# A planner that keeps a clock for the DMAs, and splits a loaded piece of weights by it

## The chip, the cores and the metric

The kernel runs on one core of one Trainium2 chip. The metric is device time in microseconds (us) of one execution. Times of before come from three timed runs and one profiled execution.

## The reference, cut to what matters

Attention with a decaying bias over 8 batches of 8 heads (576 tokens, 64 per head), and then a mixture of 8 experts on its output, 4608 rows of 512:

```python
scores = where(causal, -1e9, q @ k.T / 8 + min(-(cum_i - cum_j), 0))   # cum = cumsum(max(s, 0))
x = softmax(scores) @ v                                                # 4608 x 512
# routing: all 4608*8 logits x @ w_gate in falling order; a token goes to the expert of its largest
# logit that still has room; an expert takes cap = 576 tokens
for e in range(8):
    out[mask_e] = max(x[mask_e] @ w1[e], 0) @ w2[e]      # w1[e] 512 x 1024, w2[e] 1024 x 512
```

The output is what counts; the gate's product must be exact enough that no token goes to another expert, so x and the weights are held as two f16 numbers each, a high part and a remainder.

## The kernel before, in words

The first part of the span (up to about 342 us) is attention; the change leaves it alone. Then experts follow one another, numbered here 1 to 8 in the order in which they fill up (the code's `j` is 0 to 7).

One expert computes in two halves. In the h half TensorE multiplies the gathered, transposed rows `xT` by `w1p` into `ph` (128x512, line 1109) and `pht` (128x64, line 1113): 96 pairs of one of each. ScalarE makes `hT` from it (line 1117), VectorE its remainder (1126). In the y half TensorE multiplies `hT` by `w2p` into `py` (lines 1146 and 1137), ScalarE copies `y` out (1148), and GpSimd writes it to the output by a scatter (`out_dram`, line 1158), five per expert.

While one expert computes, the next is prepared:

- The routing search and the places of its tokens, a chain of small VectorE instructions and small TensorE matmuls (`cnt`, lines 870 to 900) that goes back and forth between the two. It ends in `iw` (which rows of the weights) and `ids` (which rows of x).
- The weights come in 12 pieces by indirect DMAs that GpSimd issues (line 1051, tile `wst`): 4 of `w1` (128x1024 f32, 0.52 MB) and 8 of `w2` (128x512 f32, 0.26 MB). A piece is then split: ScalarE makes the high part (`hi`, line 1055), VectorE the remainder (`lo`, line 1059). There are four buffers for pieces of w1 and five for those of w2; a buffer is free after `lo`.
- The rows of x come by five indirect DMAs (`xg`, line 1075, the gathers), and each is turned by a transposing DMA that SyncE issues (`xT`, line 1078).

All engines take their instructions in a fixed order, which a planner writes while the program is built. `Clock` (line 1179) holds a planned time for TensorE (`t`), ScalarE, VectorE and GpSimd. `use(eng, dt)` adds work to an engine; `after(eng, dt, lag, f)` adds work and puts `f` on a list of things that are due `lag` later; `tick` moves `t` on with each matmul and calls what is due. What is called is recorded at that place of its engine's order, so due times set the order, and no instruction waits for a planned time on the chip: it waits for its data, its buffer, and the instructions ahead of it on its engine.

`load(j, k)` (line 1253) issues piece k of an expert and makes its `hi` due by line 1269: 1.25 us of GpSimd's planned time, and then `LAT = 7.5` us. `hi` puts the remainders on the list `spare`, from which the main loop takes one when VectorE has room. `fetch(j)` (line 1281) is asked between matmuls. It issues the five gathers when `ids` is there; else the next piece, if a buffer is planned to be free (line 1295). After the gathers it holds the w2 pieces of an expert that isn't computing yet for `HOLD = 11.0` us. `scatter` (line 1155) takes 1.1 us of GpSimd's planned time.

Of the kernel before, what the change touches and what calls it, by code (L numbers as in the profile page):

```python
# [55 lines left out]
class Attention:  # L56
    def __init__(self, tc, ctx, qT, kT, vN, sN, wg, xs, nb, L, router=None):
        self.router = router
        self.tc, self.nc = tc, tc.nc
        self.qT, self.kT, self.vN, self.sN, self.wg, self.xs, self.L = qT, kT, vN, sN, wg, xs, L  # L60
        self.nb = nb
        P = lambda name, bufs, **k: ctx.enter_context(tc.tile_pool(name=name, bufs=bufs, **k))
        self.P = P
        self.c = P("ac", 1)
        self.dr = P("adr", 1, space=DRAM)
        self.st = {}
# [643 lines left out]
SLATE = -1.0  # L710
PACE = 1.7
GPACE = 1.3
HOLD = 11.0
PLEAD = 0.7
LAT = 7.5
NW = (4, 5)
HOP = -0.6
AHEAD = 0.5
# [306 lines left out]
class Moe:  # L1025
# [62 lines left out]
    def units(self, xT, w1p, w2p, ids, clock, f0=0, turn=()):  # L1088


        nc = self.nc
        h = {}

        def start():
            h["h"] = self.p.tile([128, 8, 2, 512], F16, name="hT", bufs=1)
            h["r"] = self.p.tile([128, 8, 2, 64], F16, name="hR", bufs=1)
            h["t"] = self.ps_t.tile([128, 8, 64], F32, name="pht", tag="pt")

        def mm1(f, c, k, tiles=None):
            if "h" not in h:  # L1100
                start()
            if f not in h:
                h[f] = self.ps.tile([128, 4, 128], F32, name="ph", tag="ps")
            ph, pt = h[f], h["t"]
            a, b = ((0, 0), (0, 1), (1, 0))[k]
            w = w1p[:, c, a, 128 * f:128 * f + 128]
            first, last = c == 0 and k == 0, c == 3 and k == 2
            if tiles is None:
                nc.tensor.matmul(ph, w, xT[:, 0:4, 4 * b + c], start=first, stop=last)  # L1109
            elif tiles < 4:  # L1110
                nc.tensor.matmul(ph[:, tiles], w, xT[:, tiles, 4 * b + c], start=first, stop=last)  # L1111
            if tiles in (None, 4):
                nc.tensor.matmul(pt[:, f], w, xT[:, 4, 4 * b + c, 0:64], start=first, stop=last)  # L1113
            if last and tiles in (None, 3):
                hT = h["h"]
                p2 = ph.rearrange("p i t -> p (i t)")
                nc.scalar.activation(hT[:, f, 0], p2, AF.Relu)  # L1117
                clock.after("a", 0.45, RLATE, lambda: lo(p2, hT[:, f, 1], hT[:, f, 0]))
                if f == 7:
                    hR = h["r"]  # L1120
                    nc.scalar.activation(hR[:, :, 0], pt, AF.Relu)
                    clock.after("a", 0.45, RLATE, lambda: lo(pt, hR[:, :, 1], hR[:, :, 0]))

        def lo(ps, o, hi):
            clock.use("v", 0.65)
            nc.vector.scalar_tensor_tensor(o, ps, 0.0, hi, op0=OP.max, op1=OP.subtract)  # L1126

        def mm2(i, f, k):
            n = 128 if i < 4 else 64
            if i == f == k == 0:  # L1130
                h["y"] = self.p.tile([128, 5, DM], F32, name="y")
            if f == k == 0:
                h["py"] = self.ps.tile([128, DM], F32, name="py", tag="ps")
            py, hT, y = h["py"], h["h"], h["y"]
            if i == 4:

                nc.tensor.matmul(py, h["r"][:, f].rearrange("p a t -> p (a t)"), w2p[:, f, k],  # L1137
                                 start=(f == 0 and k == 0), stop=(f == 7 and k == 1))
                if f == 7 and k == 1:
                    t = self.p.tile([64, DM], F32, name="t")  # L1140
                    nc.scalar.activation(t, py[64:128], AF.Copy, scale=YSC)
                    clock.after("a", 0.45, 0.2, lambda: fold(y, py, t))
                return
            a, b = ((0, 0), (0, 1), (1, 0))[k]
            first, last = f == 0 and k == 0, f == 7 and k == 2
            nc.tensor.matmul(py, hT[:, f, a, 128 * i:128 * i + n], w2p[:, f, b], start=first, stop=last)  # L1146
            if last:
                nc.scalar.activation(y[:, i], py, AF.Copy, scale=YSC)  # L1148
                clock.after("a", 0.45, SLATE, lambda: scatter(y, n, i))

        def fold(y, py, t):
            nc.vector.scalar_tensor_tensor(y[:64, 4], py[0:64], YSC, t, op0=OP.mult, op1=OP.add)
            clock.after("v", 0.65, SLATE, lambda: scatter(y, 64, 4))

        def scatter(y, n, i):
            clock.use("p", 1.1)
            nc.gpsimd.memset(self.spacer, 0.0)
            st = nc.gpsimd.indirect_dma_start(  # L1158
                out=self.out, out_offset=bass.IndirectOffsetOnAxis(ap=ids[:n, i:i + 1], axis=0),
                in_=y[:n, i], in_offset=None)  # L1160
            for s in self.scat:
                self.tc.declare_no_dep(st.ins, s.ins, reason="other rows")
            self.scat.append(st)

        us = [(0.47, f) for f in turn[:1]]
        for i in range(5 if f0 else 0):
            us += [(0.47, f) for f in turn[i + 1:i + 2]]

            us += [(0.058 if i < 4 else 0.03, lambda i=i, f=f, c=c, k=k: mm1(f, c, k, i))
                   for ks in (((0, 1), (2,)) if i == 0 else (range(3),))  # L1170
                   for f in range(f0) for k in ks for c in range(4)]
        us += [(0.245, lambda f=f, c=c, k=k: mm1(f, c, k)) for f in range(f0, 8) for c in range(4) for k in range(3)]
        n1 = len(us)
        us += [(0.216, lambda i=i, f=f, k=k: mm2(i, f, k))
               for i in (0, 1, 2, 4, 3) for f in range(8) for k in range(3 if i < 4 else 2)]
        return us, n1


class Clock:


    def __init__(self):
        self.at = dict(t=0.0, a=0.0, v=0.0, p=0.0)
        self.late = []

    @property
# [4 lines left out]
    def use(self, eng, dt):  # L1191
        self.at[eng] = max(self.at[eng], self.t) + dt
        return self.at[eng]

    def after(self, eng, dt, lag, f):

        self.late.append((self.use(eng, dt) + lag, f))
# [17 lines left out]
def route_and_experts(tc, ctx, R, xs, w1, w2, out):  # L1215
# [3 lines left out]
    clock = Clock()  # L1219
# [33 lines left out]
    def load(j, k):  # L1253

        u = info[j]["wu"][k]

        def hi():
            clock.after("a", u[1](), 0.1, lambda: spare.extend(parts))

        def lo(i):  # L1260
            clock.use("v", u[2][i]())
            if i + 1 == len(u[2]):
                now["out"][k > 3] -= 1
                info[j]["left"].discard(k)

        parts = [lambda i=i: lo(i) for i in range(len(u[2]))]
        u[0]()
        now["out"][k > 3] += 1
        clock.after("p", 1.25, LAT, hi)


    spare = []
# [1 line left out]
    def wait():  # L1274

        if spare:
            spare.pop(0)()
        else:
            clock.wait()

    def fetch(j, force=False):

        d = info[j]
        if "weights" in d and "w1p" not in d:
            d["w1p"], d["w2p"], d["wu"] = M.weights(d["weights"])
            d["left"], d["next"] = set(range(12)), 0
        if "ids" in d and "xT" not in d:
            d["xT"], d["xu"] = M.gather(d["ids"])
        if d.get("xu"):
            for f in d["xu"]:  # L1290
                clock.use("p", GPACE)
                f()
            d["xu"], d["hold"] = [], clock.t + HOLD
            return GPACE * 5
        free = lambda: now["out"][d["next"] > 3] < NW[d["next"] > 3]

        early = j > now["j"] and (not d.get("hold") or clock.t < d["hold"])
        if "wu" in d and d["next"] < 12 and not (early and d["next"] > 3) and (free() or force):
            while not free():
                wait()  # L1300
            load(j, d["next"])
            d["next"] += 1
            return PACE
        return None
# [7 lines left out]
    d = info[0]  # L1312
# [20 lines left out]
    for j in range(E):  # L1333
        d = info[j]
# [22 lines left out]
        if j + 1 < E:  # L1357
            d = info[j + 1]
            while "ids" not in d:
                if not step(streams[1], True):  # L1360
                    step(streams[0], True)

            while d.get("xu", True) or d["left"] & set(range(4)):
                if not fetch(j + 1):
                    wait()
# [53 lines left out]
```

## Time and profile before

| | us |
|---|---|
| timed runs, median (lowest to highest) | 862.95 (859.68 to 864.87) |
| the profiled execution, its own time | 858.84 |
| its span, first to last instruction | 857.1 |
| TensorE busy in the span | 761.5 (89%) |
| VectorE, GpSimd, ScalarE busy | 613.0, 478.4, 387.0 |

The mean granted clock of TensorE is 0.942 of full speed. A row of a timeline gives start, duration, engine, line, operation, tiles and count, and in brackets the idle time before it and what ended it. PE is TensorE, DVE VectorE, ACT ScalarE, POOL GpSimd, SP SyncE.

### The profile page before, as it was taken

The page shows a single profiled execution, that of the slowest core. Times are in us where ns is not written, and L with a number is a line of the kernel's source. Part 1 is how long each engine was busy: PE and PEld are TensorE (multiplying, and loading weights), DVE is VectorE, ACT ScalarE, POOL GpSimd, SP SyncE. Part 2 cuts the span into 40 slices and gives each one's busy share as a digit, 9 for nine tenths or more (in the row PEclk, how much of TensorE's full clock was granted, in tenths as well). Part 3 has the DMA queues.
Part 4 walks back from the last instruction along what each step waited for, and adds up shares of the span by engine and source line. Part 5 has one row for each costly group of instructions (what it writes and reads, how often), then busy time and mean ns, then how long its engine had stood idle before and what let it go on. Part 6 is the DMA issues. An engine that isn't in the chain of part 4 may idle for free.

```text
span 857.1 us, 22612 instructions
## 1 busy us (share of the span) xinstructions
PE 761.5 (89%) x9241; PEld 482.7 (56%) x9241; DVE 613.0 (72%) x1578; ACT 387.0 (45%) x866; POOL 478.4 (56%) x587
## 2 busy tenths in 40 slices
PE   8887899989889998269989999998989969959996
PEld 3576777877777787147545455454444525424442
DVE  6789999999999978668768878776677737115110
ACT  5466778878768787024213333231232113214110
POOL 5577899999989996062353534633462342432101
PEclk9689999999999999589999999999998979969999
DMA  6865999898988806052393837546283290491001
GB/s 176 249 178 151 198 238 236 207 236 234 232 205 223 177 31 141 33 187 67 114 188 103 223 101 194 151 134 169 81 211 107 95 221 28 125 210 62 31 13 43
DMA packets 122222, 128.69 MB, mean 150 GB/s; under 512 B 79781, under 2 KB 88329, under 8 KB 122118
## 3 DMA queue, kind: packets, MB, share of 16 engines
q1 hardware_dynamic: 103938, 74.31, 37.1%
q0 software_dynamic: 15744, 52.46, 20.3%
q8 instruction: 72, 1.18, 0.6%
q10 hardware_dynamic: 2436, 0.48, 0.3%
q14 instruction: 32, 0.26, 0.1%
HBM read 71.99 MB, written 19.49 MB: 107 GB/s over the span
## 4 chain that ended last, share of the span: by engine, by line
PE 48%; DVE 24%; issue 12%; DMA 5%; POOL 5%; ACT 3%; another core or an unknown queue 1%; ACTq 0%; SPq 0%; POOLq 0%; DVEq 0%
PE py L1146 15%; PE ph L1109 15%; DVE mr L297 7%; DVE R L393 3%; PE pht L1113 2%; PE py L1137 2%; DVE K L267 2%; DVE Vl L267 2%; PE ph L1111 2%; PE cnt L883 2%; POOL R L393 2%; PE pi L1013 1%; DVE Q L267 1%; DMA md<-mt 1%; DMA Q<-Q 1%
## 5 line engine op out<-in xcount | busy, mean ns | idle before, releaser
L393 POOL TENSOR_TENSOR R<-P 128x512 f16<-128x512 f32 x158 | 195.9, 1254 | 19.3 <-ACT P L391 19.3
L1109 PE MATMUL ph<-xT,w1p 128*128 128x512 f16 x696 | 187.1, 391 | 11.8 <-issue 11.7
L1146 PE MATMUL py<-w2p,hT 128*128 128x512 f16 x768 | 177.1, 381 | 0.3 <-issue 0.3
L1051 POOL DMA_INDIRECT wst<-in_w_dram,iw x96 | 98.3, 1024 | 138.8 <-DVE iw L857 40.4
L1113 PE MATMUL pht<-xT,w1p 128*128 128x64 f16 x768 | 139.0, 195 | 8.9 <-issue 8.7
L297 DVE TENSOR_REDUCE mr<-pss 128x1 f32<-128x512 f32 (+4 forms) x224 | 133.5, 608 | 9.9 <-PE pss L305 5.7
L391 ACT ACTIVATE P<-pst 128x512 f32<-128x512 f32 (+1 forms) x224 | 120.5, 563 | 41.4 <-PE pst L384 14.6
L1158 POOL DMA_INDIRECT out_dram<-y,ids x40 | 42.7, 1068 | 155.9 <-ACT y L1148 127.2
L1109 PEld LDWEIGHTS <-w1p 128*128 128x128 f16 x696 | 69.5, 100 | 93.8 <-issue 22.5
L1146 PEld LDWEIGHTS <-hT 128*128 128x128 f16 x768 | 70.2, 98 | 81.5 <-issue 5.4
L1117 ACT ACTIVATE hT<-ph 128x512 f16<-128x512 f32 x64 | 38.1, 597 | 169.5 <-PE ph L1109 89.0
L459 PE MATMUL po<-V,R 128*128 128x65 f16 x960 | 112.9, 195 | 1.3 <-POOL R L393 1.0
L457 PE MATMUL po<-V,P 128*128 128x65 f16 x960 | 112.4, 196 | 0.9 <-DVE xf L479 0.9
L458 PE MATMUL po<-Vl,P 128*128 128x64 f16 x960 | 112.3, 194 | 0.0
L382 PE MATMUL pst<-Q,K 70*128 70x64 f16 (+4 forms) x512 | 104.7, 253 | 4.3 <-ACT P L391 3.0
L384 PE MATMUL pst<-Q,K 128*128 128x64 f16 (+4 forms) x512 | 105.4, 253 | 0.0
L1126 DVE SCALAR_TENSOR_TENSOR hT<-ph,hT 128x512 f16<-128x512 f32 x64 | 43.8, 687 | 84.9 <-ACT hT L1117 54.4
L457 PEld LDWEIGHTS <-P 128*128 128x128 bf16 x960 | 91.1, 99 | 5.6 <-issue 0.2
L303 PE MATMUL pss<-K,Q 67*128 67x512 f16 (+3 forms) x256 | 72.5, 311 | 22.8 <-DVE mr L297 19.6
L459 PEld LDWEIGHTS <-R 128*128 128x128 f16 x960 | 90.3, 98 | 1.8 <-POOL R L393 1.5
L458 PEld LDWEIGHTS <-P 128*128 128x128 bf16 x960 | 90.2, 100 | 1.1 <-issue 1.0
L1113 PEld LDWEIGHTS <-w1p 128*128 128x128 f16 x768 | 71.3, 99 | 12.9 <-issue 12.2
(223 smaller groups left out, 1562.7 us busy)
## 6 DMA issues: line engine op xcount, KB each, us to landing
rq<-in_q_dram SPq DMA_DIRECT2D x32, 288.0 KB
rk<-in_k_dram SPq DMA_DIRECT2D x32, 288.0 KB
rv<-in_v_dram SPq DMA_DIRECT2D x32, 288.0 KB
Q<-Q SPq DMA_DIRECT2D x62, 144.0 KB
K<-K SPq DMA_DIRECT2D x62, 144.0 KB
xs<-xp SPq DMA_DIRECT2D x32, 256.0 KB
wst<-in_w_dram,iw POOLq DMA_INDIRECT x96
xs<-xp SPq DMA_DIRECT2D x8, 128.0 KB
```

The lines of the kernel that those rows point to most:

```text
L297: nc.vector.tensor_reduce(o, ps, AX.X, OP.max)
L382: nc.tensor.matmul(ps[:, c0:c0 + n], K[0:70, 0, par, pr, ks], Q[0:70, 0, pr, par, q0:q0 + n], start=True, stop=False)
L384: nc.tensor.matmul(ps[:, c0:c0 + n], K[:, 1, par, pr, ks], Q[:, 1, pr, par, q0:q0 + n], start=False, stop=not diag)
L391: nc.scalar.activation(P[:, c0:c0 + n], ps[:, :n], AF.Exp, scale=1.0 / YS)
L393: self.post(lambda: eng.tensor_tensor(R[:, c0:c0 + n], P[:, c0:c0 + n], strided_hi(P)[:, c0:c0 + n], op=OP.subtract), T["RT"][0 if gp else 1])
L457: nc.tensor.matmul(po[:, i, :], H[:, c:c + 128], V[:, pr, sl, :], start=f, stop=False)
L458: nc.tensor.matmul(po[:, i, 0:64], H[:, c:c + 128], Vl[:, pr, sl, :], start=False, stop=False)
L459: nc.tensor.matmul(po[:, i, :], R[:, c:c + 128], V[:, pr, sl, :], start=False, stop=l)
L1051: nc.gpsimd.indirect_dma_start(out=t, out_offset=None, in_=src, in_offset=bass.IndirectOffsetOnAxis(ap=iw[:, k:k + 1], axis=0))
L1109: nc.tensor.matmul(ph, w, xT[:, 0:4, 4 * b + c], start=first, stop=last)
L1113: nc.tensor.matmul(pt[:, f], w, xT[:, 4, 4 * b + c, 0:64], start=first, stop=last)
L1146: nc.tensor.matmul(py, hT[:, f, a, 128 * i:128 * i + n], w2p[:, f, b], start=first, stop=last)
```

## The change

The planner gets a fifth clock, `d`, for the DMAs. Each piece, gather and scatter adds a cost to it: 2.6 us for a piece of w1, 1.4 for one of w2, 3.0 for a gather, 1.0 for a scatter, starting at 2.0 us after the planned time or when `d` is through with what came before. The `hi` of a piece is due at the later of two times: 6.0 us after the planned time at which it is issued, or 3.5 us after `d` is through with it. The hold after the gathers is 10.0 us in place of 11.0. No instruction is added or taken away; what changes is their order on the engines.

```diff
-HOLD = 11.0
+HOLD = 10.0
 PLEAD = 0.7
-LAT = 7.5
+LAT = (6.0, 3.5)
+DMA = dict(w1=2.6, w2=1.4, x=3.0, y=1.0)
...
         def scatter(y, n, i):
             clock.use("p", 1.1)
+            clock.dma("y")
...
-        self.at = dict(t=0.0, a=0.0, v=0.0, p=0.0)
+        self.at = dict(t=0.0, a=0.0, v=0.0, p=0.0, d=0.0)
...
+    def dma(self, what):
+
+        self.at["d"] = max(self.at["d"], self.t + 2.0) + DMA[what]
+        return self.at["d"]
...
         u[0]()
         now["out"][k > 3] += 1
-        clock.after("p", 1.25, LAT, hi)
+        clock.use("p", 1.25)
+        clock.late.append((max(clock.t + LAT[0], clock.dma("w2" if k > 3 else "w1") + LAT[1]), hi))
...
             for f in d["xu"]:
                 clock.use("p", GPACE)
+                clock.dma("x")
                 f()
             d["xu"], d["hold"] = [], clock.t + HOLD
```

Nine lines are added above some of the code, so line 1051 is 1052 in the new file, 1055 is 1056, 1075 is 1076, 1117 is 1118 and 1158 is 1160.

GpSimd while expert 4 computes and expert 5 is fetched: before,

```order
L1051 DMA wst<-in_w_dram,iw 128x1024 x4
L1075 DMA xg<-xs,ids 128x1024 x4
L1075 DMA xg<-xs,ids 64x1024
L1051 DMA wst<-in_w_dram,iw 128x512 x4
L1157 MEMSET spacer 1x1
L1158 DMA out_dram<-y,ids 4608x512
L1051 DMA wst<-in_w_dram,iw 128x512 x2
```

and in the changed kernel, at the same place of the same engine:

```order
L1052 DMA wst<-in_w_dram,iw 128x1024 x4
L1076 DMA xg<-xs,ids 128x1024 x4
L1076 DMA xg<-xs,ids 64x1024
L1052 DMA wst<-in_w_dram,iw 128x512 x2
L1159 MEMSET spacer 1x1
L1160 DMA out_dram<-y,ids 4608x512
L1052 DMA wst<-in_w_dram,iw 128x512 x3
```

Between the gathers and the first scatter of expert 4 stand two pieces of w2 in place of four; the others stand behind the scatter.

GpSimd while expert 6 computes and expert 7 is fetched: before,

```order
L1051 DMA wst<-in_w_dram,iw 128x1024 x2
L1075 DMA xg<-xs,ids 128x1024 x4
L1075 DMA xg<-xs,ids 64x1024
L1051 DMA wst<-in_w_dram,iw 128x1024 x2
L1051 DMA wst<-in_w_dram,iw 128x512 x3
L941 MEMSET X 128x40
L1051 DMA wst<-in_w_dram,iw 128x512 x2
L1157 MEMSET spacer 1x1
L1158 DMA out_dram<-y,ids 4608x512
```

and in the changed kernel:

```order
L1052 DMA wst<-in_w_dram,iw 128x1024 x4
L1076 DMA xg<-xs,ids 128x1024 x4
L1076 DMA xg<-xs,ids 64x1024
L1052 DMA wst<-in_w_dram,iw 128x512 x4
L942 MEMSET X 128x40
L1052 DMA wst<-in_w_dram,iw 128x512
L1159 MEMSET spacer 1x1
L1160 DMA out_dram<-y,ids 4608x512
```

Two pieces of w1 have moved from behind the gathers to in front of them: five pieces follow the gathers in place of seven.

ScalarE in the h half of expert 1 (`w2p` is a `hi`, `hT` an h tile): before,

```order
L1055 ACTIVATE w2p<-wst 128x512
L1117 ACTIVATE hT<-ph 128x512 x3
L1055 ACTIVATE w2p<-wst 128x512 x2
L1117 ACTIVATE hT<-ph 128x512
L1055 ACTIVATE w2p<-wst 128x512 x2
L1117 ACTIVATE hT<-ph 128x512
L1055 ACTIVATE w2p<-wst 128x512
L1117 ACTIVATE hT<-ph 128x512 x2
L1121 ACTIVATE hR<-pht 128x8x64
```

and in the changed kernel:

```order
L1056 ACTIVATE w2p<-wst 128x512
L1118 ACTIVATE hT<-ph 128x512 x2
L1056 ACTIVATE w2p<-wst 128x512
L1118 ACTIVATE hT<-ph 128x512
L1056 ACTIVATE w2p<-wst 128x512 x2
L1118 ACTIVATE hT<-ph 128x512
L1056 ACTIVATE w2p<-wst 128x512
L1118 ACTIVATE hT<-ph 128x512 x3
L1122 ACTIVATE hR<-pht 128x8x64
```

The last `hi` stands one h tile earlier than before.

## Rows read from the trace of the kernel before

**Rows 1.** The page's head, and the engines' busy time.

```profile
span 857.1 us, 22612 instructions
...
PE 761.5 (89%) x9241; PEld 482.7 (56%) x9241; DVE 613.0 (72%) x1578; ACT 387.0 (45%) x866; POOL 478.4 (56%) x587
```

**Rows 2.** Waits from 390 to 857 us: total us, times, longest.

```profile
PE cnt L891 <- DVE ca L887: 7.5, 5, 3.3
...
ACT w1p L1055 <- DMA wst<-in_w_dram,iw: 2.3, 1, 2.3
...
ACT w2p L1055 <- DMA wst<-in_w_dram,iw: 1.1, 1, 1.1
```

**Rows 3.** Windows, TensorE alone: the last h half, then four stretches of fetching.

```profile
core 0: us, PE busy (x), PEclk, DMA share, GB/s
803.00:823.00 20.00, 20.00 (x165) 1.00 0.04 14
583.00:589.00 6.00, 3.45 (x19) 0.90 1.15 301
638.00:650.00 12.00, 7.54 (x47) 0.72 0.91 187
691.00:708.00 17.00, 10.42 (x50) 0.70 1.07 218
751.00:770.00 19.00, 10.33 (x49) 0.64 1.08 220
```

**Rows 4.** Timeline of GpSimd while expert 5 is fetched: gather, first and last piece.

```profile
574.88 1.09 POOL L1075 DMA_INDIRECT xg<-xs,ids  x1 [4.22 <-DVE ids L1020]
...
581.57 0.97 POOL L1051 DMA_INDIRECT wst<-in_w_dram,iw  x1 [0.30 <-issue]
...
585.37 0.96 POOL L1051 DMA_INDIRECT wst<-in_w_dram,iw  x1 [0.30 <-issue]
```

**Rows 5.** The same for expert 6: first and last piece behind the gathers.

```profile
636.56 0.97 POOL L1051 DMA_INDIRECT wst<-in_w_dram,iw  x1 [0.30 <-DMA xg<-xs,ids]
...
642.09 0.96 POOL L1051 DMA_INDIRECT wst<-in_w_dram,iw  x1 [0.30 <-issue]
```

**Rows 6.** The same for expert 7.

```profile
690.49 0.97 POOL L1051 DMA_INDIRECT wst<-in_w_dram,iw  x1 [0.30 <-issue]
...
698.09 0.96 POOL L1051 DMA_INDIRECT wst<-in_w_dram,iw  x1 [0.31 <-issue]
```

**Rows 7.** The same for expert 8.

```profile
748.84 0.97 POOL L1051 DMA_INDIRECT wst<-in_w_dram,iw  x1 [0.30 <-issue]
...
758.93 0.96 POOL L1051 DMA_INDIRECT wst<-in_w_dram,iw  x1 [0.30 <-issue]
```

**Rows 8.** The same for expert 4: the piece behind the gathers, scatter, next piece.

```profile
531.32 1.00 POOL L1051 DMA_INDIRECT wst<-in_w_dram,iw  x1 [0.30 <-issue]
...
536.62 1.11 POOL L1158 DMA_INDIRECT out_dram<-y,ids  x1 [4.21 <-ACT y L1148]
538.04 0.97 POOL L1051 DMA_INDIRECT wst<-in_w_dram,iw  x1 [0.30 <-issue]
```

**Rows 9.** Window of that stretch, all engines; columns as Rows 3, each engine.

```profile
524.00:540.00 16.00, 15.80 (x110) 7.74 (x108) 14.97 (x44) 4.77 (x7) 9.04 (x10) 1.00 0.83 190
```

**Rows 10.** Timeline of SyncE: the five transposes for expert 4, then expert 8.

```profile
528.05 9.12 SPq L1078 DMA_TRANSPOSE xT<-xg  x5
...
745.87 12.02 SPq L1078 DMA_TRANSPOSE xT<-xg  x5
```

**Rows 11.** Timelines: a late w2 piece, issued by GpSimd, its `hi` on ScalarE.

```profile
659.91 1.26 POOL L1051 DMA_INDIRECT wst<-in_w_dram,iw  x1 [0.35 <-DVE ca L887]
...
665.04 0.63 ACT L1055 ACTIVATE w2p<-wst 128x512 f16<-128x512 f32 x1 [1.09 <-DMA wst<-in_w_dram,iw]
```

**Rows 12.** Timeline of TensorE in the stretch of expert 8.

```profile
757.68 0.21 PE L1113 MATMUL pht<-xT,w1p 128*128 128x64 f16 x1 [2.65 <-issue]
758.41 0.58 PE L1109 MATMUL ph<-xT,w1p 128*128 128x512 f16 x1 [0.52 <-issue]
```

## The prediction, made before the changed kernel ran

> **What bounds the kernel now.** I read the page's busy shares first: TensorE is busy for 761.5 of 857.1 us, the next engine for 613.0 [rows 1]. Then the waits of the experts' part. The change deals with the moment at which a landed piece is split, so the first question is whether anything waits for a piece now. Hardly: ScalarE stood for 2.3 us at one piece of w1 and for 1.1 us at one of w2 in the whole stretch from 390 us on, and TensorE waited for VectorE's `ca`, which stands in one queue with the remainders of the pieces, 7.5 us in 5 waits [rows 2]. Pieces are split after they have landed. What the change can give is therefore not in the split itself, but in what the split's due time moves: when buffers are planned free, and so the order of GpSimd's DMAs.
>
> So I looked for where TensorE loses time, with windows of TensorE alone. In the last h half, when nothing is fetched any more, it makes 165 matmuls in 20.00 us without a gap, at a clock of 1.00: 0.121 us each (the first window of [rows 3]). The four other windows are stretches in which the next expert is fetched. At 0.121 us their 19, 47, 50 and 49 matmuls would have taken 2.3, 5.7, 6.1 and 5.9 us; they lasted 6, 12, 17 and 19 us. That is 3.7, 6.3, 10.9 and 13.1 us lost, 34 us together. Part of it is the granted clock, which falls there to means of 0.90 down to 0.64, that is to the lower of its two levels (1.2 GHz) for a while after TensorE has stood; the larger part is that TensorE stands. It doesn't stand for a semaphore: the timeline says "issue" before such matmuls, with 2.65 us of idle time in the middle of a run of equal matmuls [rows 12].
>
> What do the four stretches share? GpSimd issues weight pieces without a break right behind the five gathers, while SyncE's transposes of the gathered rows run (9.12 us for the five of expert 4, 12.02 for those of expert 8 [rows 10]). Behind the gathers stand four pieces for expert 5 (581.57 to 585.37 [rows 4]), five for expert 6 (636.56 to 642.09 [rows 5]), seven for expert 7 (690.49 to 698.09 [rows 6]) and nine for expert 8 (748.84 to 758.93 [rows 7]). At 0.26 MB for a piece of w2 and 0.52 for one of w1 that is 1.05, 1.31, 2.36 and 3.41 MB, so 3.5, 4.8, 4.6 and 3.8 us lost per MB. For expert 4 only one piece (0.26 MB) follows before GpSimd stands at the scatter until 536.62 [rows 8], and TensorE is busy for 15.80 of 16.00 us at a clock of 1.00 although the DMAs are 0.83 busy [rows 9]. I read this as: weight pieces that follow the gathers into the transposes cost TensorE about 4.4 us per MB, and one small piece costs nothing. That is an inference from five stretches; nothing in the trace names the mechanism.
>
> **The change part by part.** No instruction goes or comes, so TensorE's own work is the same, and the sum is one of stretches.
>
> *Expert 5's fetch.* The first scatter of expert 4 now stands behind two pieces, not four; it holds GpSimd until the first `y` is there, and the other pieces go after the transposes. 0.52 MB remain. By the rate that is 2.3 us, by the nearest stretch, that of expert 4, nothing. I take 1.3, the middle: a gain of 2.4 us (1.4 to 3.7).
>
> *Expert 7's fetch.* Two pieces of w1 (1.05 MB) go ahead of the gathers. Five of w2, 1.31 MB, follow; this is the very order that expert 6's fetch has before, where 6.3 us are lost. Against it: the same nine pieces and five gathers still stand in one row, and the loss could stay at 10.9. I go by the nearest row, 6.3: a gain of 4.6 us (0 to 6.3).
>
> *Expert 4's fetch.* Before, one piece stands ahead of the first scatter, now none, with three behind it, as before. The scatter comes when `y` is there, at about 536.6 us [rows 8]; the transposes are all issued by 537.2 (528.05 + 9.12 [rows 10]). Here the cover is thin: if the gathers come some 3 us later, because the search's chain on VectorE has other remainders in it, the three pieces fall into the last transposes. 0.79 MB times 4.6 is 3.6 us at most, nothing at the least; I take 1.0.
>
> *Other fetches.* Expert 8's keeps its nine pieces behind the gathers and its 13.1 us; expert 6's keeps its five. For expert 2 a scatter goes ahead of the gathers, for expert 3 one piece of w2 goes ahead of them; neither puts more behind them. I cost these at nothing (1 us to either side). The pieces of w2 that now go after scatters are needed only in the next expert's y half, an h half of over 20 us later; that hides them.
>
> *The earlier split.* Where the DMA clock is idle, a `hi` is due 6.9 us after the issue (2.0 + 1.4 + 3.5), and not 8.75 (1.25 + 7.5): 1.85 us earlier, as ScalarE's order for expert 1 shows. A late piece of w2 was issued at 659.91 and its `hi` began at 665.04, after a wait of 1.09 us [rows 11]: 5.1 us after the issue it had only just landed. With 1.85 us less, some `hi` will reach ScalarE before their piece. Behind one stand evictions of `ph` and `py`, of which TensorE has four buffers, and its remainder on VectorE with the search behind it. At the least this costs nothing, since the waits are shorter than a tile's 2.9 us (12 pairs at 0.242) and four buffers cover them; at the most it doubles TensorE's 7.5 us of waiting for `ca` [rows 2]. Most of it is covered, so I take 1.0.
>
> *Behind the gathers the opposite holds*: five gathers put 15 us on the DMA clock, so a `hi` is due later than before. The weights have an h half to spare, so nothing waits; buffers come free later, which is what moves the pieces above.
>
> The Trainium skill speaks against my reading. Its page "SBUF — State Buffer", section "Who interferes with whom", says that DMAs have ports of their own, and that a DMA never contends with a compute engine. By that rule TensorE's standing cannot be the doing of the pieces, moving them gives nothing, and the sum would be the 1.0 us of early splits, 864 us. The rows do not agree on the face of it: with DMA shares of 0.91 to 1.15 TensorE loses 34 us in four stretches, with 0.04 none [rows 3]. But with 0.83 it loses nothing either [rows 9].
>
> The sum: -2.4 - 4.6 + 1.0 + 1.0 = -5.0 us. Against the profiled execution (858.84 us; its span of 857.1 and 1.7 around it) that is 853.8. The median of the timed runs lies 4.1 above that execution, so I set the sum against the median: 862.95 - 5.0, or 858 us.
>
> **The rivals.**
>
> 1. *No change.* What stalls TensorE is not the number of pieces behind the gathers but the whole row of DMAs of a fetch, which keeps its bytes: nine pieces and five gathers for expert 7, before and after. Or it is something that only coincides. For it: the rates per MB scatter from 3.5 to 4.8, and 0.83 of DMA share goes without loss. Against: four stretches stand in the order of their bytes. The split alone then changes nothing, since only 3.4 us of waits hang on it. Time: 862.95 + 0 to 2 us of early splits, 863 to 865. The rule of the Trainium skill above ("SBUF — State Buffer") would end here too.
>
> 2. *The early split becomes the new wait (slower).* The place is ScalarE's and VectorE's queues in the y halves, where the pieces that go between the scatters have no gather before them in the DMA clock: about three per expert, 24 in all. If a piece lands later than 6.9 us after its planned issue, `hi` holds ScalarE, the remainder holds VectorE, and the search behind it holds TensorE's `cnt` matmuls. It decides if GpSimd runs more than 1.8 us behind its plan there (6.9 less 5.1). Price: for six experts whose search still runs, 18 pieces at 0.6 us (a third of the 1.85), 11 us, against a gain of 5: 869. For it: one piece was late already. Against: four ph/py buffers, and ScalarE is busy for 45%, VectorE for 72% of the span [rows 1].
>
> 3. *More than forecast.* Expert 5's loss goes altogether (3.7), expert 7's down to expert 5's (7.2), expert 4 and the splits cost nothing: -10.9, or 852.
>
> **How the numbers follow.** Two measurements of this kernel differ by 0.5% (4.3 us) without a change, so faster is below 858.6 and slower above 867.3. My forecast has 0.48, with 855 to 862 as its own range, and lies on the bound: 0.26 of it faster, 0.22 the same. Rival 1 has 0.25: 0.22 same, 0.03 slower. Rival 2 has 0.13: 0.11 slower, 0.02 same. Rival 3 has 0.14, faster. Together faster 0.40, same 0.46, slower 0.14. The range that leaves out 2 in 10 goes from 851 (rival 3) to 866 (most of rival 1, the beginning of rival 2).
>
> **What would show it.** TensorE's windows in the fetches of experts 5 and 7: about 1 and 6 us lost in place of 3.7 and 10.9, those of experts 6 and 8 as they were. If the fetch of expert 7 still loses 10 us, rival 1 is right. If ScalarE's waits for `wst` rise from 3.4 us to over 15, and TensorE's for `ca` with them, rival 2 is. If expert 4's fetch, clean before, shows a clock below 1.00, its term was too small. I am wrong as a whole if the time moves while these windows keep their losses.

## The result, and the profile after

| | before | after |
|---|---|---|
| timed runs, median (lowest to highest), us | 863.23 (859.63 to 865.84) | 866.78 (863.06 to 873.60) |
| ratio, 95% interval | | 1.0048, 1.0028 to 1.0069 |
| profiled execution, its span, us | 857.1 | 862.4 |

The changed kernel is 0.5% slower where 858 us were forecast. The profiled execution shows 5.3 us more, 1.7 more than the medians. The head of its page:

```profile
span 862.4 us, 22621 instructions
## 1 busy us (share of the span) xinstructions
PE 763.2 (88%) x9241; PEld 483.1 (56%) x9241; DVE 611.8 (71%) x1578; ACT 387.8 (45%) x866; POOL 479.9 (56%) x587
```

The same work, and a little more standing. First the places that the prediction named: windows of TensorE alone, the last h half and then the fetches of experts 5, 6, 7 and 8 (columns as in [rows 3]).

```profile
808.00:828.00 20.00, 20.00 (x167) 1.00 0.04 14
596.00:602.00 6.00, 4.34 (x33) 1.00 1.15 286
646.00:658.00 12.00, 7.57 (x52) 0.84 0.92 213
703.00:716.00 13.00, 9.73 (x57) 0.87 1.12 221
757.00:770.00 13.00, 4.93 (x19) 0.61 1.11 308
```

Expert 5's fetch keeps its clock and has one short stand, expert 7's stands less (3.3 us without a matmul where [rows 3] has 6.6), experts 6 and 8 stand as before. To see the whole account, cut the experts' part into halves, from the first matmul of a half to the first of the next, read from the timelines. The search's small matmuls between two halves count with the later one; the last half ends where its last matmul starts. "After, again" is a second profile of the changed kernel from a later run, "third chip" one of the kernel before on another chip; both are experiments told below.

| us | before | after | after, again | before, third chip |
|---|---|---|---|---|
| up to expert 1's first h matmul | 380.3 | 383.0 | 385.2 | 381.4 |
| expert 1: h, y | 32.5, 33.3 | 35.9, 34.0 | 31.6, 32.1 | 29.2, 27.6 |
| expert 2 | 29.9, 26.7 | 29.6, 26.3 | 34.0, 27.1 | 29.5, 25.9 |
| expert 3 | 27.6, 27.7 | 29.6, 30.4 | 31.2, 28.6 | 27.1, 26.1 |
| expert 4 | 29.5, 29.1 | 26.6, 29.8 | 26.6, 29.1 | 26.8, 26.9 |
| expert 5 | 33.7, 27.0 | 34.4, 27.6 | 33.2, 27.0 | 25.9, 26.9 |
| expert 6 | 37.0, 25.8 | 32.8, 25.9 | 33.1, 25.9 | 25.8, 25.8 |
| expert 7 | 36.8, 24.2 | 36.2, 24.2 | 34.6, 24.2 | 23.5, 24.2 |
| expert 8 | 23.5, 24.0 | 23.5, 24.0 | 23.5, 24.0 | 23.5, 24.0 |

Expert 5 is fetched in the h half of expert 4, which is 2.9 us shorter; expert 7 in that of expert 6, 4.2 us shorter. These gains are there. Against them stand 8.1 us in experts 1 to 3 (177.7 before, 185.8 after), 2.7 ahead of them, where no instruction has moved, and 1 to 2 us in small change.

Where is the loss in expert 3? Timelines of the changed kernel, at the end of GpSimd's work for that expert (GpSimd alone) and then TensorE and VectorE in it; expert 3's h half began at 508.9:

```profile
505.19 0.93 POOL L1160 DMA_INDIRECT out_dram<-y,ids  x1 [1.97 <-DVE ca L888]
509.02 0.97 POOL L1052 DMA_INDIRECT wst<-in_w_dram,iw  x1 [2.90 <-DVE ca L888]
...
512.88 0.96 POOL L1052 DMA_INDIRECT wst<-in_w_dram,iw  x1 [0.30 <-issue]
```

```profile
512.70 0.19 PE L1114 MATMUL pht<-xT,w1p 128*128 128x64 f16 x1
...
514.85 0.19 DVE L888 CAST ca<-cnt 128x32 f16<-128x32 f32 x1 [2.43 <-remote]
514.96 0.68 DVE L1060 SCALAR_TENSOR_TENSOR w2p<-wst,w2p 128x512 f16<-128x512 f32 x1
515.09 0.24 PE L892 MATMUL cnt<-ca,qb 128*128 128x8 f16 x4 [2.20 <-DVE ca L888]
```

Read the last line with care. It puts TensorE's 2.20 us down to VectorE's `ca`. But `ca` itself waited 2.43 us, for the `cnt` matmuls that TensorE had begun from 511.99 to 512.22. TensorE stood, `ca` waited for it, and the wait row names the victim. The trace's semaphore records bear this out: TensorE's signal for those matmuls is recorded at 514.83, 2.4 us after their modelled end, and `ca` starts 0.02 us later. Late signals go with the stands: from 380 us on, 51 of 301 of TensorE's signals come over 0.1 us after the modelled end of the matmul that gives them, and 2 of 315 in the profile of the third chip, told below.

The stand comes while GpSimd issues the last three pieces of expert 3 and a scatter of expert 2. Before, the last of these began at 503.86, 1.1 us into the h half. Now the first of the pieces waits 2.90 us; its buffer is the one whose remainder is done at 508.75, when the h half begins; before, the same remainder was done at 496.72, 6 us ahead of it.

Nor is it the early split. ScalarE's waits for pieces, and TensorE's for `ca`, in the waits from 390 us on (columns as in [rows 2]):

```profile
PE cnt L892 <- DVE ca L888: 5.1, 3, 2.2
...
ACT w1p L1056 <- DMA wst<-in_w_dram,iw: 2.2, 2, 1.3
...
ACT w2p L1056 <- DMA wst<-in_w_dram,iw: 1.7, 2, 0.9
```

3.9 us at pieces after 3.4, and 5.1 at `ca` after 7.5.

### The profile page after: what moved, and what is told of

It reads as the page before. It is cut to its first block, busy times and chain, and to the rows that moved or that the text cites. A ratio compares the mean times of both kernels' runs of the same rounds, so it can differ in the third digit from the quotient of the medians.

```text
span 862.4 us, 22621 instructions
## 1 busy us (share of the span) xinstructions
PE 763.2 (88%) x9241; PEld 483.1 (56%) x9241; DVE 611.8 (71%) x1578; ACT 387.8 (45%) x866; POOL 479.9 (56%) x587
## 3 DMA queue, kind: packets, MB, share of 16 engines
q1 hardware_dynamic: 103938, 74.31, 35.9%
## 4 chain that ended last, share of the span: by engine, by line
PE 42%; DVE 27%; issue 14%; POOL 5%; DMA 4%; ACT 4%; another core or an unknown queue 2%; SPq 1%; ACTq 0%; POOLq 0%; DVEq 0%
PE py L1147 13%; PE ph L1110 12%; DVE mr L297 9%; DVE R L393 4%; DVE Vl L267 3%; DVE K L267 2%; PE pht L1114 2%; PE ph L1112 2%; PE cnt L884 2%; PE py L1138 2%; POOL out_dram L1160 1%; DVE Q L267 1%; PE pi L1014 1%; POOL wst L1052 1%
## 5 line engine op out<-in xcount | busy, mean ns | idle before, releaser
L1147 PE MATMUL py<-w2p,hT 128*128 128x512 f16 x768 | 179.3, 384 | 1.1 <-issue 1.1
L1110 PEld LDWEIGHTS <-w1p 128*128 128x128 f16 x696 | 69.0, 99 | 90.2 <-issue 18.5
L1149 ACT ACTIVATE y<-py 128x512 f32<-128x512 f32 x32 | 19.1, 598 | 134.8 <-PE py L1147 111.6
```

## Experiments: what makes TensorE stand

The prediction read the stands as the work of weight pieces beside the transposes. In expert 8 nothing is fetched, so its halves (23.5 and 24.0 us without a stand) are a clean bench. Each kernel below is the changed kernel with DMAs added there, into buffers that nobody reads.

**Nine pieces twice, plain DMAs, gathers alone, all together.**

```diff
+        for k in range(9):
+            n, src = (FF, M.w1) if k < 4 else (DM, M.w2)
+            t = M.st[n].tile([128, n], F32, name="wst")
+            tc.nc.gpsimd.indirect_dma_start(out=t, ..., in_=src, ...)   # x1_pieces, x4_both
+            tc.nc.sync.dma_start(out=t, in_=src[128 * k:128 * k + 128]) # x3_plain
+        for f in M.gather(d["ids"])[1]: f()                             # x2_rows, x4_both (ahead)
...
+            if j == E - 1 and n in (30, n1 + 2): extra(d)
```

> The changed kernel, with nine more DMAs of GpSimd in expert 8, where nothing is fetched any more: the row that expert 8's fetch has behind its gathers (four pieces of w1, five of w2, 3.41 MB), once in expert 8's h half and once in its y half, into buffers that nobody reads; no gathers and no transposes with it. Without it these halves last 23.5 and 24.0 us. Theory A, the prediction's reading (pieces cost TensorE time when they run beside the transposes): under 1 us lost in either half. Theory B (a long row of GpSimd's DMAs costs TensorE time in an h half, where it issues 192 matmuls in 23.4 us, and not in a y half with 112): 6 to 13 us lost in the h half, under 1.5 in the y half. Theory C (the bytes alone, whatever the half): about the same loss of 5 to 13 us in both.

> The changed kernel, with five more gathers and their five transposes in each half of expert 8, read by nobody, and no pieces. Theory A: under 1 us lost in either half, since no pieces follow. Theory B: 0 to 3 us in the h half (five DMAs are a short row), under 1 in the y half. A theory D, that the transposes alone are what costs, wants 3 us and more in the h half.

> As the run with nine pieces, but the nine are plain DMAs that SyncE issues, same sizes and destinations. If the bytes are what costs, the h half loses what it lost with GpSimd's row (to 30%). If it is that GpSimd issues them, with addresses from a table, under 1.5 us.

> The changed kernel, with the whole row of expert 8's fetch (five gathers with their transposes, then nine pieces) in each half of expert 8. Theory A: 12 to 15 us lost in the h half and as much in the y half. Theory B: 12 to 15 in the h half, under 3 in the y half. Theory C: both halves lose what the nine pieces alone lose, and some more for the gathers.

Nothing holds GpSimd or SyncE there, so both sets of GpSimd's were issued in the h half: 18 pieces, 10 gathers, 28 DMAs. SyncE, which is free earlier, issued its 18 plain DMAs from 789.77 to 813.05, that is from the y half of expert 7 into the h half of expert 8. The h halves took 39.8, 30.8, 23.5 and 53.3 us, the y halves 24.0 each. So the halves are not compared yet, but three things are settled. Windows of the run with 18 pieces, all engines (busy and count of PE, PEld, DVE, ACT, POOL, then clock, DMA share, GB/s):

```profile
806.90:816.40 9.50, 9.50 (x78) 4.82 (x76) 1.38 (x2) 1.19 (x2) 7.37 (x8) 1.00 0.85 279
816.40:832.00 15.60, 4.30 (x16) 1.42 (x16) 0.69 (x1) 0.60 (x1) 9.89 (x12) 0.59 0.84 286
834.00:844.00 10.00, 10.00 (x75) 5.02 (x74) 2.19 (x4) 1.79 (x3) 0.00 (x0) 0.89 0.00 0
```

The pieces begin at 806.90. At the same DMA share TensorE first runs without a gap for 9.5 us and 8 DMAs, then makes 16 matmuls in 15.6 us until the row has landed. There is no transpose and no gather in it: theory A falls. The run with plain DMAs:

```profile
808.00:822.00 14.00, 14.00 (x107) 7.07 (x106) 2.08 (x3) 2.39 (x4) 1.84 (x4) 1.00 0.81 297
```

The same bytes at the same rate cost nothing, here and in expert 7's y half (24.2 us, as without them). And the gathers alone, their row, and the end of their transposes:

```profile
809.40:819.50 10.10, 10.10 (x84) 5.04 (x81) 1.38 (x2) 1.19 (x2) 7.67 (x8) 1.00 0.74 175
819.50:827.00 7.50, 3.11 (x14) 1.12 (x14) 0.81 (x2) 1.08 (x2) 2.90 (x4) 0.70 1.27 211
832.00:838.00 6.00, 6.00 (x51) 3.17 (x50) 1.38 (x2) 1.19 (x2) 0.00 (x0) 1.00 0.92 171
```

The transposes at a share of 0.92 cost nothing; the row of gathers does, from its ninth DMA on. Neither bytes nor transposes, then, but GpSimd's DMAs in a row. Whether it is that GpSimd issues them, or that their addresses come from a table, these runs don't tell apart: no run has plain DMAs issued by GpSimd.

**The other half, and breaks in the row.** In the first, the row of the y half stands behind the first scatter, which waits for `y`; in the second, the nine of the h half are in groups of three, with 4.4 us of memsets between.

```diff
+            if j == E - 1 and n in (30, n1 + 36): extra(d, n > n1)      # y1: 9 in h; 5 gathers + 9 in y
+            if k in (3, 6) and not y:                                   # y2: 3 + 3 + 3 in h; 9 in y
+                for _ in range(12): tc.nc.gpsimd.memset(M.pause, 0.0)   # 128x256 f32
```

> The changed kernel, with a row of nine more pieces (four of w1, five of w2) in expert 8's h half, and in its y half, behind the first scatter, which holds GpSimd until the half has begun, a row of fourteen (five gathers with their transposes, nine pieces). In the run with eighteen pieces GpSimd issued all of them in the h half; TensorE ran on for 9 us (eight DMAs at 1.27 us) and then stood until the row had landed. Theory B (a row longer than some eight DMAs costs TensorE time in an h half only): 4 to 8 us lost in the h half (23.5 us without it), under 1.5 us in the y half (24.0 without). Theory C (any long row, whatever the half): 4 to 8 in the h half, 8 to 14 in the y half. Theory A (the prediction's): nothing in the h half, 8 and more in the y half, where transposes run.

> As that run, but the nine in the h half in three groups of three, with 3 to 4 us of memsets by GpSimd between the groups; in the y half a row of nine pieces without gathers. If the unbroken row is what costs (theories B and C): under 1 us lost in the h half, though the bytes are the same. If the bytes in an h half cost: 4 to 8 us again. In the y half theory B wants under 1 us, theory C 4 to 8.

Measured: h 28.5, y 32.1 us in the first; h 23.5, y 24.0 in the second. The first (h half, its stand; y half, its stand):

```profile
807.00:817.30 10.30, 10.30 (x85) 5.26 (x83) 1.39 (x2) 1.19 (x2) 7.86 (x9) 1.00 0.74 248
817.30:822.00 4.70, 2.04 (x10) 0.77 (x9) 0.00 (x0) 0.61 (x2) 1.76 (x3) 0.90 0.72 243
840.70:857.00 16.30, 16.30 (x76) 7.30 (x75) 0.00 (x0) 1.19 (x2) 12.37 (x13) 1.00 0.87 217
857.00:866.00 9.00, 2.46 (x7) 0.65 (x6) 0.00 (x0) 0.59 (x1) 4.15 (x7) 0.78 1.13 271
```

and the second, the h half with its groups, the y half with its nine and three scatters, and one of the breaks:

```profile
811.00:832.00 21.00, 21.00 (x175) 10.88 (x172) 4.84 (x7) 4.18 (x7) 16.27 (x34) 1.00 0.51 166
838.40:853.00 14.60, 14.60 (x69) 6.63 (x68) 0.00 (x0) 1.20 (x2) 11.38 (x14) 1.00 0.77 256
```

```profile
813.60 0.95 POOL L1324 DMA_INDIRECT wst<-in_w_dram,iw  x1 [0.31 <-issue]
814.54 4.40 POOL L1323 MEMSET pause<- 128x256 f32 x12
819.10 0.95 POOL L1324 DMA_INDIRECT wst<-in_w_dram,iw  x1 [0.15 <-issue]
```

Theory B falls as well: the y half also stands, only later, after 13 DMAs and 16.3 us. Count the instructions. Each row is opened by a scatter (in the run with 18 pieces at 805.62, which adds 11+11 to that window). From there to the stand TensorE had issued 89+87, 84+81 and 85+83 matmuls and weight loads in the h halves, 76+75 in the y half: 151 to 176 each time, in 10.1 to 16.3 us. With 69+68 there was no stand, and with breaks none after 347. So the reading that is left, the *row theory*: while GpSimd issues DMAs without a break, TensorE gets through some 150 to 175 instructions and then stands, mostly until the row is over. An h half issues them faster than a y half and has room for a shorter row.

The count isn't a rule for every row. Three rows of the changed kernel in experts 2 and 3, from their first DMA to the stand, or, for the first, to the row's end:

```profile
483.60:503.10 19.50, 19.10 (x116) 8.86 (x114) 16.08 (x47) 4.91 (x7) 15.80 (x16) 1.00 0.97 176
509.02:512.90 3.88, 3.87 (x44) 2.12 (x43) 2.87 (x8) 1.63 (x3) 3.05 (x5) 1.00 0.42 136
544.79:552.10 7.31, 7.27 (x56) 3.54 (x55) 5.59 (x15) 0.60 (x1) 5.87 (x7) 1.00 0.95 237
```

The first has thirteen DMAs, 1.5 us apart and not 1.27, and no stand in 230 instructions. The others stand after 87 and 111; their rows begin 2.90 and 2.33 us after the work before them. A break of 4.4 us was enough in expert 8; that breaks of 2 to 3 us don't start the count anew would fit, but no run varies the break, and what fixes the count is open.

**A hold that breaks the rows.** If that is right, the w2 pieces of the next expert should not follow the gathers at all; between the scatters of the y half each scatter's wait is a break.

```diff
         def scatter(y, n, i):
+            clock.first += i == 0
...
-        early = j > now["j"] and (not d.get("hold") or clock.t < d["hold"])
+        early = j > now["j"] and (not d.get("hold") or clock.t < d["hold"] or clock.first <= now["j"])
```

> The changed kernel, in which the w2 pieces of the next expert are also held until the first scatter of the expert that computes is in GpSimd's order. So no piece of w2 follows the gathers in an h half; they stand between the scatters, which wait for the y half. For expert 8 a row of nine is left (five gathers, four pieces of w1). Theory B: the h halves of experts 5, 6 and 7, which lose 8.7, 7.4 and 12.8 us in the changed kernel, lose 2, 3 and 6; 18 us less in all, 847 to 852 us. Theory C: what goes from the h halves comes back in the y halves, 860 to 868. A new wait (w2 pieces late for their y half): over 868.

> The same hold in the kernel before. Its h halves of experts 4 to 7 lose 3.8, 8.2, 11.5 and 13.3 us. Theory B: 1, 2, 4 and 6 are left, so 24 us less, 838 to 845. Theory C: 858 to 866. If theory B holds and the change is only another shuffle of the same rows, the two kernels with the hold differ by less than 5 us.

Measured: 848.24 us, 0.9803 of before (0.9770 to 0.9837), and 844.01, 0.9770 (0.9732 to 0.9808). Both are faster than either kernel of the case. In the profile of the second the h halves of experts 4 to 7 take 27.1, 26.6, 26.1 and 28.7 us (29.5, 33.7, 37.0, 36.8 before), and 6.5 us come back in the y halves of experts 4 to 6, whose rows are now longer. Expert 7's h half keeps a row of ten (a scatter, five gathers, four pieces of w1) and its stand, 3.0 us and a clock of 0.86 in the second of these windows, all engines:

```profile
729.80:740.00 10.20, 10.16 (x84) 5.09 (x82) 2.68 (x4) 2.00 (x4) 7.84 (x8) 1.00 0.73 175
740.00:752.00 12.00, 8.99 (x57) 4.16 (x58) 3.27 (x5) 2.89 (x5) 1.98 (x3) 0.86 1.03 246
```

## Experiments: the parts of the change, and another chip

```diff
 p_early, on before:   -LAT = 7.5    +LAT = 5.65
 p_late, on after:     due = max(clock.at["p"] + 7.5, clock.dma(...) + LAT[1]);  HOLD = 11.0
 p_from4, on after:    due as after if now["j"] > 2 else clock.at["p"] + 7.5
 g2_before, on the hold:  before the first piece behind the gathers of a fetch, in an h half:
+            clock.use("p", 4.0)
+            for _ in range(12): tc.nc.gpsimd.memset(M.pause, 0.0)
```

> One part of the change alone, on the kernel before: every split due 6.9 us after its issue (LAT 5.65 in place of 7.5), no DMA clock, so no later split behind the gathers; hold 11. Row theory (what costs is an unbroken row of GpSimd's DMAs, once TensorE has issued some 150 instructions since its start): the order of expert 1's h half is that of the changed kernel, so its 2.8 us are lost here too; expert 5's fetch has two pieces behind the gathers, expert 6's three, expert 7's five (before 4, 5, 7), so the h halves of experts 4, 5 and 6 gain 3, 3 and 4; with nothing lost in expert 3: 855 to 860 us. The prediction's rival 2 (early splits become the wait): over 866.

> The other part alone: the due time of before, unless the DMA clock is later (so only splits behind gathers and scatters move, and only to a later time); hold 11. Row theory: expert 1 as before; experts 2 and 3 lose what the changed kernel loses there (the h and y half of expert 3: 2 and 2 to 3 us), since the buffers come free later and the last pieces and scatters of a y half slip into the next h half; experts 4 and 6 gain 3 and 4 in their h halves: 859 to 863. If the late splits have no part in the loss: 855 to 858.

> The changed kernel, with the due time of before while experts 1 to 3 compute, and the new one from expert 4 on. If the gain in the h halves of experts 4 and 6 (7 us) is real and was given back in experts 1 and 3, this kernel keeps it: 855 to 859 us. If the change gains nothing and the halves only differ from run to run: 862 to 867.

> The kernel before with the hold until the first scatter (844 us), and 4 us of memsets on GpSimd between the gathers and the next piece where that still follows in an h half (experts 1, 7 and 8). Row theory: the h half of expert 7, which loses 5.3 us with the hold alone, loses under 1, that of expert 1 some 2 us less than its 32.6: 836 to 841. If a pause between gathers and pieces does nothing: 842 to 847. If GpSimd's memsets are paid for by VectorE or delay the pieces until the y half waits: over 847.

These four ran on the third chip, and there the kernel before took 810.44 us. They measured 1.0083 (1.0053 to 1.0113), 0.9986 (0.9955 to 1.0017), 0.9988 (0.9964 to 1.0012) and 0.9999 (0.9980 to 1.0018). The question was no longer which part, but where 52 us were lost on the others. The next runs put the changed kernel beside its parts:

> The changed kernel itself, unedited, beside its parts. On a chip where TensorE stands in the rows (before at about 863 us): 1.003 to 1.007 of before, with its losses again in experts 1 and 3 and its gains in the h halves of experts 4 and 6. On a chip where it doesn't (before at about 810): the rows cost nothing, nothing can be gained from them, and only the new waits are left: 1.000 to 1.008.

> The early split alone (on a chip without the standing it was 1.008 of before, 815 us). Where TensorE stands in the rows: its halves of expert 1 as in the changed kernel (35 us, before 32.5), those of experts 4 to 6 3, 3 and 4 us shorter than before: 0.991 to 0.998 of before. If it loses in its own right everywhere: 1.003 and more. Without the standing: 1.005 to 1.011 again.

> The late split alone (0.999 without the standing). Where TensorE stands in the rows: expert 1 as before (32.5 us), expert 3 as in the changed kernel (h 29.6, y 30), experts 4 and 6 3 and 4 us shorter in the h half: 0.995 to 1.002. Without the standing: 0.996 to 1.002 again.

> The new due times from expert 4 on alone (0.999 without the standing). Where TensorE stands in the rows: expert 1 to 3 as before, the gain of the h halves of experts 4 and 6 kept: 0.989 to 0.997. If it is 0.998 or more there, the gain of those fetches was never real. Without the standing: 0.996 to 1.002 again.

This was a chip with the long times again (before 860.60): 0.9982 (0.9956 to 1.0008), 0.9936 (0.9908 to 0.9964), 0.9959 (0.9930 to 0.9987), 1.0025 (0.9996 to 1.0054). The last two asked for the kernel before on the same footing:

> The kernel before, unedited, for a second profile. From the first matmul of expert 1 to the end of expert 3 it took 177.7 us in the profile that the prediction read, and 178.9 with the hold until the first scatter, while ten profiles with the changed order there took 185 to 191. If the loss in experts 1 to 3 is the change's: 176 to 181 again (where TensorE stands in the rows). If it is chance: 182 or more. Without the standing: 162 to 164, which tells nothing of it.

> Hold until the first scatter and 4 us of memsets between gathers and pieces. Without the standing it made no difference (0.9999). Where TensorE stands in the rows: expert 7's h half under 25 us (36.8 before, 28.7 with the hold alone), and 0.965 to 0.975 of before, 832 to 841 us. If the pause does nothing there: 0.977 as the hold alone.

They came to the third chip: before 810.29, its profile in the table above; the hold with breaks 0.9992 (0.9970 to 1.0014). So the break between gathers and pieces is untested where it could show. But the profile of the unedited kernel on the third chip settles more than it was asked. GpSimd's row in expert 8's fetch, and windows of TensorE alone over the fetches of experts 5 to 8:

```profile
705.92 0.97 POOL L1158 DMA_INDIRECT out_dram<-y,ids  x1 [3.27 <-ACT y L1148]
707.19 0.99 POOL L1075 DMA_INDIRECT xg<-xs,ids  x1 [0.30 <-issue]
...
723.91 0.95 POOL L1051 DMA_INDIRECT wst<-in_w_dram,iw  x1 [0.30 <-issue]
```

```profile
565.00:577.00 12.00, 12.00 (x97) 1.00 0.97 192
616.00:628.00 12.00, 12.00 (x116) 1.00 1.14 182
665.00:677.00 12.00, 12.00 (x99) 1.00 1.14 253
712.00:731.00 19.00, 19.00 (x149) 1.00 1.08 265
```

The same fifteen DMAs in 18 us, spaced as before, DMA shares up to 1.14, and TensorE doesn't miss a matmul. Its 48.6 us less of span lie in the halves of experts 1 to 7: 12.3 in experts 1 to 3, 37.3 in 4 to 7. On this chip the stands don't exist, so neither the hold nor the late split has anything to gain there.

What the parts say where TensorE stands: the early split alone makes expert 5's h half 26.5 us (three pieces behind the gathers; 33.7 before), gives most of that back in its y half (33.2 us; 27.0 before), and is faster as a whole, so by itself it isn't the loss; the late split alone is faster too. But it was expected to lose in expert 3, and did not (27.8 and 28.7 us), so the changed kernel's loss there is not the late split's alone either. `p_from4` fell short of its expectation: its fetch of expert 5 still has four pieces behind the gathers, as before, and expert 4's h half takes 29.1 us, as before. And its experts 1 to 3 take 183.8 us, with due times of before; `p_late`'s take 182.3, the early split's 184.5, nine profiles with the changed kernel's order there 184.6 to 190.7, and two with the order of before up to expert 4's fetch 177.7 and 178.9. Expert 1's h half took 32.5 and 32.7 us in these two, 34.6 and 34.5 in `p_late` and `p_from4`, which have the same order of GpSimd's DMAs there. So part of what experts 1 to 3 lost is the change's: expert 3's h half takes 29.6 to 31.3 us in all nine profiles of its order, with a stand of 2.1 to 2.2 us in each, always 6.1 or 6.2 us into it, and 27.6 and 28.2 us in the two of the order of before, without a stand there. (The changed kernel has no profile on the third chip, where the same order could be seen without stands.) And part varies from run to run: expert 1's h half takes 35.9 us and 31.6 in two profiles of one kernel. How much of each stays open. The hold's own part (10.0 us in place of 11.0) has no run of its own: the late split alone also has the hold of before.

## Why the prediction was wrong, point by point

**The reading of the stretches** ("weight pieces that follow the gathers into the transposes cost TensorE about 4.4 us per MB"). That TensorE stands there for no semaphore was right, and so, about, was its size: 34 us in four stretches, and on the third chip, where the stands are missing, the halves of experts 4 to 7 are 37.3 us shorter. The cause was wrong. Where TensorE stands, transposes cost nothing, bytes cost nothing, an unbroken row of GpSimd's DMAs does. The measure per MB worked by accident, since more pieces make a longer row (the four rates average 4.2, not 4.4; that moves the sum by 0.1 us). Rival 1 had this half right ("the whole row of DMAs of a fetch"), but drew from it that nothing would move.

**Experts 5 and 7** (-2.4 and -4.6). Measured -2.9 and -4.2, and -2.9 and -3.9 in the other profile of the changed kernel. The windows above lose about what the prediction said would show it: 1.7 us without a matmul for expert 5 (1 forecast) and, at 0.121 us for each of 57 matmuls, 6.1 of 13.00 for expert 7 (6 forecast). By the row theory, what helped expert 7 is the break of 3.4 us that the gathers' wait for `ids` now makes behind four pieces, so that the row is ten DMAs and not twelve.

**Expert 4's fetch** (+1.0, at most 3.6). The y half of expert 3 is 2.7 us longer. Not transposes: they are all issued by 547.55, and TensorE stands from 552.1 on. Before, GpSimd waited 4.2 us at the first scatter [rows 8] and again at the second; now it waits 2.33 at the first and hardly at the second, and seven DMAs follow one another from 544.79. Before, the second scatter, and then both of the changed kernel:

```profile
543.60 1.00 POOL L1158 DMA_INDIRECT out_dram<-y,ids  x1 [1.95 <-ACT y L1148]
```

```profile
544.79 1.42 POOL L1160 DMA_INDIRECT out_dram<-y,ids  x1 [2.33 <-ACT y L1149]
...
550.58 1.01 POOL L1160 DMA_INDIRECT out_dram<-y,ids  x1 [0.21 <-issue]
```

That the lost break made this stand is a reading; no run tests it.

**The earlier split** (+1.0; rival 2). Nothing in the waits. One thing stays open: on the third chip the early split alone is 0.8% slower, and the profile, taken of its fastest run, doesn't show where.

**"Other fetches ... I cost these at nothing (1 us to either side)".** This is the step that failed. Beside the three fetches above the profile has +9.7 us, 5.4 of them in experts 1 to 3. I had looked at the pieces behind the gathers of late experts only, and wrote of the later splits that "the weights have an h half to spare, so nothing waits". The weights had; the rows had not: pieces and a scatter that had been done at the h half's beginning now fell into it, and TensorE stood beside them (512.7 to 514.9, in each of nine profiles of this order). That accounts for some 2 us; what the rest of the 5.4 is stays open. 2.7 of the 9.7 lie ahead of any moved instruction, and that stretch runs from 380.3 to 385.2 us over the profiles, so they are no cost of the change.

**The sum.** -5.0 forecast, +5.3 in the profile, +3.6 between the medians. Timed again on a chip with stands, the ratio was 0.998 (0.9956 to 1.0008), no difference. So the 0.5% is a measured fact of that comparison and didn't recur: a gain of some 7 us and a loss of about the same size, both, as the traces read, made of stands that depend on where rows happen to break.

The Trainium skill's "SBUF — State Buffer", section "Who interferes with whom", lets TensorE wait on nobody. The plain DMAs and the third chip agree; GpSimd's rows on the other chips do not (4.30 us busy of 15.60 in the run with 18 pieces). What TensorE waits for in them, no run shows.

## What to carry to other kernels

Where GpSimd issues indirect DMAs beside a busy TensorE, look at how many follow one another without a wait, not at their bytes, and put breaks into long rows by queueing them behind waits that are there anyway: it was worth 2.0 and 2.3% here where TensorE stood. Idle time marked "issue" in a run of equal matmuls was TensorE's own standing here, and a wait of its search chain in the same microseconds can be the same stand under another name. Time a small change more than once, and on more than one chip, before explaining half a per cent.

## What was not expected of the hardware

The later runs name three chips. On two of them the kernel before takes 860.6 to 862.9 us, on the third 810.4, in one and the same program, while DMA spacing, DMA shares and the unhindered halves (24.2, 23.5, 24.0 us) agree. On which chip the first comparison ran isn't on record; its times are those of the two. And in expert 8's rows TensorE's stand goes by its own instructions rather than by time: 151 to 176 of them fit into a row before it, whether this takes 10.1 us or 16.3; beside other rows it stands earlier or not at all (after 87 and 111, and not in 230). Loading of its instructions isn't what it waits for by the trace: in the run with 18 pieces one such load of 16 KB began at 817.3, after the stand had begun at 816.4, and took 1.0 us, the next began at 847.6, and the stand lasted until 832. Every timed run on record has a span and a granted clock beside its time, so no run shows the kernels unobserved; whether the observing has a part in the stands is not tested.
